# Loading a 4 KB input through the ACT queue, so that the SP queue begins with the first weights

## The chip, the cores and the metric

One core of one Trainium2 chip. The metric is the device time of one execution in microseconds (us). In the profile, PE multiplies matrices, VectorE (DVE), ACT and POOL compute, and SP and ACT issue transfers (loads), each into a queue of its own, called its ring below. Sixteen DMA engines carry them out in packets; here a packet is one row of a load, or the small mark that says it is complete. A semaphore is a counter on which an engine waits until a load or another engine has raised it. The kernel before takes 1297.78 us (median of 6 runs beside the changed kernel, 1297.59 to 1297.96).

## The reference

A decode step with one new token for each of four sequences: layernorm of x (4 x 512), an attention block over a cache, and a SwiGLU feed-forward block, all summed.

```python
xn = _layernorm(x, axis=-1)
q = (xn @ wq).reshape(B, Sq, H, Dh).transpose(0, 2, 1, 3)        # B 4, Sq 1, H 32, Dh 128
p = softmax(einsum("bhqd,bhkd->bhqk", q, k_cache) * Dh ** -0.5)   # 8192 keys for each head
a = einsum("bhqk,bhkd->bhqd", p, v_cache)...reshape(B, Sq, H * Dh) @ wo
return x + a + (silu(xn @ w_gate) * (xn @ w_up)) @ w_down
```

The caches are 2 x 4 x 32 x 8192 x 128 in bf16, some 537 MB. Each is read once, so the work is a long read from memory.

## The kernel before

The parts that matter, with cuts marked by `# ...`. `load_k` and `load_v` take 2 MB each, into one of nine buffers of a ring.

```python
x_sb = persist.tile([B, D], dt.bfloat16, name="x_sb")
nc.sync.dma_start(out=x_sb[:], in_=x_flat[:, :])
wq_v = A_wq.rearrange("(p c) n -> p c n", c=EC)
wq_t = []
for c2 in range(0, EC, 2):                       # two loads of 2 MB
    t_ = slot()
    nc.sync.dma_start(out=t_[:].rearrange("p (c n) -> p c n", c=2), in_=wq_v[:, c2:c2 + 2, :])
    wq_t.append(t_)
# ...
load_k(0)
load_k(1)
# ... ident, ident_f
for z_ in zq:
    nc.gpsimd.memset(z_[:], 0.0)                 # two long fills on POOL
# ...
nc.vector.tensor_copy(out=xf[:], in_=x_sb[:])    # the first use of x
# ... layernorm on VectorE, with one square root on ACT
nc.scalar.activation(out=std[:], in_=vsum[:], func=ACT.Sqrt, bias=epst[:, 0:1], scale=1.0 / D)
# ... transpose of xn; q = xn @ wq, first with wq_t[0], then with wq_t[1]
for i in range(M + LP + 1):                      # M = 128 pairs of head and sequence
    if i + 2 < M:
        load_k(i + 2)
    if 0 <= i + 2 - LP < M:
        load_v(i + 2 - LP, parts=4 if i + 2 - LP == M - 1 else 1)
    # ... scores of k tile i, softmax once a head, p @ v of tile i - 4
# ...
nc.sync.dma_start(out=out_flat[:, :], in_=res[:])
```

## Time and profile before

| | before |
|---|---|
| time, median | 1297.78 us |
| span of the profiled run | 1295.9 us |
| bytes read by DMA | 550.8 MB |
| DMA rate in the middle slices | some 430 GB/s |
| busy: PE, VectorE, ACT | 85%, 54%, 4% |
| first issue of wq on SP | 1.16 us |
| first wq data | 2.14 us |
| output issued by SP | 1293.59 us |

The first wq data are read from the DMA rate in slices of 0.02 us: a slice counts the packets that start in it, and the first that shows 16 KB packets starts at 2.14:

```profile
2.12:2.14 0.02, 0.00 (x0) 0.00 (x0) 0.02 (x1) 0.00 (x0) 0.02 (x1) 1.00 0.00 0
2.14:2.16 0.02, 0.00 (x0) 0.00 (x0) 0.02 (x1) 0.00 (x0) 0.02 (x1) 1.00 14.57 3277
```

### The profile page before, as it was taken

The page shows a single profiled execution, that of the slowest core. Times are in us where ns is not written, and L with a number is a line of the kernel's source. Part 1 is how long each engine was busy: PE and PEld are TensorE (multiplying, and loading weights), DVE is VectorE, ACT ScalarE, POOL GpSimd, SP SyncE. Part 2 cuts the span into 40 slices and gives each one's busy share as a digit, 9 for nine tenths or more (in the row PEclk, how much of TensorE's full clock was granted, in tenths as well). Part 3 has the DMA queues.
Part 4 walks back from the last instruction along what each step waited for, and adds up shares of the span by engine and source line. Part 5 has one row for each costly group of instructions (what it writes and reads, how often), then busy time and mean ns, then how long its engine had stood idle before and what let it go on. Part 6 is the DMA issues. An engine that isn't in the chain of part 4 may idle for free.

```text
span 1295.9 us, 11245 instructions
## 1 busy us (share of the span) xinstructions
PE 1095.1 (85%) x4676; PEld 423.2 (33%) x4676; DVE 693.3 (54%) x887; ACT 48.5 (4%) x102; POOL 5.6 (0%) x11
## 2 busy tenths in 40 slices
PE   5889888888888888888888888888888888886987
PEld 2343333333333333333333333333333333332333
DVE  7635554554554565555565455555555555544542
ACT  1000000000000000000000000000000000000000
POOL 1000000000000000000000000000000000000000
PEclk8989999999999999999999999999989989998999
DMA  9999999999999999999999999999999999999997
GB/s 396 429 430 432 431 429 431 431 431 430 430 432 430 430 430 431 431 429 432 432 428 429 434 430 429 431 431 431 431 431 431 430 430 431 430 403 419 432 429 305
DMA packets 42210, 551.49 MB, mean 426 GB/s; under 512 B 4264, under 2 KB 8368, under 8 KB 8880
## 3 DMA queue, kind: packets, MB, share of 16 engines
q1 hardware_dynamic: 42160, 550.79, 99.6%
q8 instruction: 36, 0.59, 0.2%
q14 instruction: 14, 0.11, 0.0%
HBM read 550.77 MB, written 0.00 MB: 425 GB/s over the span
## 4 chain that ended last, share of the span: by engine, by line
DMA 91%; PE 5%; DVE 3%; issue 0%; SPq 0%; ACT 0%; DVEq 0%; ACTq 0%
DMA slot<-in_A_k_cache_dram 86%; DMA slot<-in_B_w_up_dram 3%; DVE kt L256 3%; DMA slot<-in_A_v_cache_dram 3%; PE oacc L74 2%; PE sps L74 2%; PE mps L74 1%; PE xps L74 0%; SPq L97 0%; PE mps L278 0%; SPq L89 0%; DVE mx L272 0%; DVE res L388 0%; DVE yfx L227 0%; ACT o_sb L313 0%
## 5 line engine op out<-in xcount | busy, mean ns | idle before, releaser
L256 DVE STREAM_TRANSPOSE kt<-slot 128x1024 uint32<-128x1024 uint32 x512 | 593.5, 1212 | 284.8 <-DMA slot<-in_A_k_cache_dram 284.8
L74 PE MATMUL sps<-kt,zq 128*128 128x512 bf16 x2048 | 572.1, 416 | 179.0 <-DVE kt L256 165.6
L74 PEld LDWEIGHTS <-zq 128*128 128x128 bf16 x2048 | 208.8, 103 | 532.0 <-issue 361.4
L302 DVE RECIPROCAL rcp<-mps 128x4 f32<-128x4 f32 x32 | 5.8, 183 | 160.9 <-PE mps L74 160.9
L272 DVE TENSOR_REDUCE mx<-sps 128x1 f32<-128x512 f32 x32 | 22.1, 692 | 45.1 <-PE sps L74 45.1
L281 DVE TENSOR_REDUCE nm<-mps 128x4 f32<-128x64 f32 x32 | 7.2, 225 | 50.0 <-PE mps L278 50.0
L74 PE MATMUL xps<-ident_f,o_sb 128*128 128x4 f32 x256 | 33.1, 253 | 0.7 <-ACT o_sb L313 0.7
L74 PEld LDWEIGHTS xps<-ident_f,o_sb 128*128 128x128 f32 x256 | 31.1, 192 | 1.2 <-ACT o_sb L313 1.2
L247 DVE COPY zq<-qt 32x16 bf16<-32x16 bf16 x128 | 23.5, 183 | 1.3
L322 DVE TENSOR_TENSOR otn<-xps,rcp 128x4 bf16<-128x4 f32 x32 | 5.2, 162 | 34.1 <-PE xps L74 34.1
L313 ACT COPY o_sb<-oacc 128x512 f32<-128x512 f32 x32 | 18.7, 585 | 20.6 <-PE oacc L74 20.5
L74 PE MATMUL oacc<-slot,pt__1952 128*4 128x512 bf16 x64 | 14.6, 379 | 0.0
L74 PE MATMUL oacc<-slot,pt__3394 128*4 128x512 bf16 x64 | 14.6, 379 | 0.0
L74 PE MATMUL oacc<-slot,pt__6498 128*4 128x512 bf16 x64 | 14.6, 379 | 0.0
L74 PE MATMUL oacc<-slot,pt__922 128*4 128x512 bf16 x64 | 14.6, 379 | 0.0
L74 PE MATMUL oacc<-slot,pt__2158 128*4 128x512 bf16 x64 | 14.6, 379 | 0.0
L74 PE MATMUL oacc<-slot,pt__3188 128*4 128x512 bf16 x64 | 14.6, 379 | 0.0
L74 PE MATMUL oacc<-slot,pt__4424 128*4 128x512 bf16 x64 | 14.6, 379 | 0.0
L74 PE MATMUL oacc<-slot,pt__5248 128*4 128x512 bf16 x64 | 14.6, 379 | 0.0
L74 PE MATMUL oacc<-slot,pt__6282 128*4 128x512 bf16 x64 | 14.6, 379 | 0.0
L74 PE MATMUL oacc<-slot,pt__371 128*4 128x512 bf16 x64 | 14.6, 379 | 0.0
L74 PE MATMUL oacc<-slot,pt__1128 128*4 128x512 bf16 x64 | 14.6, 379 | 0.0
(204 smaller groups left out, 636.8 us busy)
## 6 DMA issues: line engine op xcount, KB each, us to landing
slot<-in_A_k_cache_dram SPq DMA_DIRECT2D x128, 2048.0 KB, 38.4
slot<-in_A_v_cache_dram SPq DMA_DIRECT2D x127, 2048.0 KB, 38.8
slot<-in_A_wq_dram SPq DMA_DIRECT2D x2, 2048.0 KB, 9.4
slot<-in_A_wo_dram SPq DMA_DIRECT2D x2, 2048.0 KB, 28.8
slot<-in_A_v_cache_dram SPq DMA_DIRECT2D x4, 512.0 KB, 28.0
slot<-in_B_w_gate_dram SPq DMA_DIRECT2D x1, 1792.0 KB, 38.2
slot<-in_B_w_up_dram SPq DMA_DIRECT2D x1, 1792.0 KB
slot<-in_B_w_down_dram SPq DMA_DIRECT2D x1, 1792.0 KB, 34.0
```

The source lines that it names most:

```text
L74: nc.tensor.matmul(out_ap, lhsT=lhsT, rhs=rhs, start=start, stop=True, skip_group_check=True, **kw)
L247: nc.vector.tensor_copy(out=zq[h % 2][a * QB:(a + 1) * QB, :, :, XO + a * QB].rearrange("p b (j r) -> p r j b", r=2), in_=qt[a * QB:(a + 1 ...
L256: nc.vector.transpose(out=kt[:].bitcast(dt.uint32).rearrange("p (j t r) -> p t j r", j=2, r=QB), in_=src.rearrange("p (t j r) -> p t j r", ...
L272: nc.vector.reduce_max(out=mx[:], in_=s_ps[h][:], axis=AX.X)
L281: nc.vector.tensor_reduce(out=nm[:], in_=mps[:, 0:P].rearrange("p (a x g r) -> p x a g r", a=NQ, x=B, r=2)[:, :, :, :, 0], axis=AX.XY, op= ...
L302: nc.vector.reciprocal(out=r_[:], in_=mps[:, P:P + B])
L313: nc.scalar.copy(out=o_sb[:], in_=o_acc[h % 2][:])
L322: nc.vector.tensor_tensor(out=otn[:, h, :], in0=xps[:], in1=rcp.pop(h)[:], op=ALU.mult)
```

## The change

The intent: SP issues its loads one after the other, and x is the first of them. The ACT queue issues nothing, and ACT isn't needed before the square root. If ACT issues x, SP can begin at once with wq, and the long stream starts sooner.

```diff
     x_sb = persist.tile([B, D], dt.bfloat16, name="x_sb")
-    nc.sync.dma_start(out=x_sb[:], in_=x_flat[:, :])
+    nc.scalar.dma_start(out=x_sb[:], in_=x_flat[:, :])
     wq_v = A_wq.rearrange("(p c) n -> p c n", c=EC)
```

## The prediction

> **What bounds the kernel now.** I began with the page's busy rows and its rows of 40 slices. The columns of the first line are engine, busy us, share of the span, instructions.
>
> ```profile
> PE 1095.1 (85%) x4676; PEld 423.2 (33%) x4676; DVE 693.3 (54%) x887; ACT 48.5 (4%) x102; POOL 5.6 (0%) x11
> ...
> DMA  9999999999999999999999999999999999999997
> GB/s 396 429 430 432 431 429 431 431 431 430 430 432 430 430 430 431 431 429 432 432 428 429 434 430 429 431 431 431 431 431 431 430 430 431 430 403 419 432 429 305
> ```
>
> No compute engine is full in every slice, but the DMA row is, at some 430 GB/s throughout. Only the first slice (396), two near the end (403, 419) and the last (305) fall short. Next the queues and the chain that ended last:
>
> ```profile
> q1 hardware_dynamic: 42160, 550.79, 99.6%
> ...
> DMA 91%; PE 5%; DVE 3%; issue 0%; SPq 0%; ACT 0%; DVEq 0%; ACTq 0%
> ```
>
> One queue carries 550.79 MB, which at 430 GB/s is 1281 us of the 1295.9 us span. The chain agrees: 91% of it is transfers. So the end is: the moment at which the data begin to flow, plus about 1281 us of stream with its few dips, plus a tail of compute. Is the stream always fed? A 2048 KB load takes a median 38.4 us from issue to landing; eight such loads at 431 GB/s need 8 x 2.097 MB / 431 GB/s = 38.9 us. So about eight loads are always outstanding, and a late issue must be later than the whole backlog before it costs anything. The list of each engine's instructions shows the same: SP's loads go round eight completion semaphores, and each waits for the one eight before it.
>
> Last, the first microseconds of the queue that the change touches (start, length, engine, line, operation):
>
> ```profile
> 0.74 0.36 SPq L84 DMA_DIRECT2D x_sb<-in_A_x_dram  x1
> 1.16 0.83 SPq L89 DMA_DIRECT2D slot<-in_A_wq_dram  x2
> 2.03 2.48 SPq L97 DMA_DIRECT2D slot<-in_A_k_cache_dram  x5
> 4.55 0.48 SPq L106 DMA_DIRECT2D slot<-in_A_v_cache_dram  x1
> 12.98 0.33 SPq L97 DMA_DIRECT2D slot<-in_A_k_cache_dram  x1
> ```
>
> and what the DMA engines moved then (the last two columns are DMA share and GB/s):
>
> ```profile
> 1.60:1.70 0.10, 0.00 (x0) 0.00 (x0) 0.10 (x1) 0.10 (x1) 0.10 (x1) 1.00 0.03 10
> 1.70:1.80 0.10, 0.00 (x0) 0.00 (x0) 0.10 (x1) 0.10 (x1) 0.10 (x2) 1.00 0.10 31
> ...
> 2.00:2.10 0.10, 0.00 (x0) 0.00 (x0) 0.07 (x1) 0.01 (x1) 0.10 (x1) 1.00 0.00 0
> 2.10:2.20 0.10, 0.00 (x0) 0.00 (x0) 0.09 (x2) 0.00 (x0) 0.10 (x1) 1.00 3.77 819
> ```
>
> The 4 KB of x pass between 1.6 and 1.8 us: 10 and 31 GB/s over 0.1 us each are 1 + 3.1 KB. The first wq data come in the slice that starts at 2.10 us, 0.94 us after that load's issue began at 1.16. Before 2.1 us the sixteen DMA engines do nothing but x. The only thing between the start and the stream that this kernel could shorten is SP's first issue.
>
> **What the Trainium skill says.** "DMA: Bandwidth & Descriptors", section "Issuing engines are not separate DMA queues", says that starting transfers from several engines only saves the sequencer's issue time, "which is usually small relative to the DMA itself". The trace gives that time: wq's issue starts 0.42 us after x's (1.16 - 0.74). That is all that this page promises here.
>
> The same page, section "Queues, rings and completion order", says that SP and ACT each have a ring on each of the same sixteen engines, and that an engine takes turns between rings packet by packet. Before, all data are on one ring, so this trace can't show it; it matters for when x lands once wq is on the other ring.
>
> "SBUF — State Buffer", section "SBUF: two separate sides", says that VectorE and GpSimd share a port pair which one instruction locks for its whole length. The trace agrees:
>
> ```profile
> 1.75 4.34 POOL L121 MEMSET zq<- 128x2528 bf16 x2
> ...
> 2.11 4.15 DVE L134 TENSOR_SCALAR rowb_q<-rowb 128x4 f32<-128x4 f32 x1
> 2.19 4.33 DVE L138 CAST xf<-x_sb 4x512 f32<-4x512 bf16 x1
> 6.55 0.67 DVE L140 TENSOR_REDUCE xsum<-xf 4x1 f32<-4x512 f32 x1
> ```
>
> An operation on 128x4 elements takes 4.15 us, and it ends just after POOL's two fills do (1.75 + 4.34 = 6.09). The cast that reads x stands behind it until 6.5.
>
> "ScalarE: Activation LUTs", section "What ACT_TABLE_LOAD costs", gives about 1283 ns for a table load; ACT's first instruction here is one of 1.28 us at 0.73.
>
> **The change part by part.** The compiled orders of the two kernels differ in one instruction: x's load leaves the head of SP's list and enters at the head of ACT's. PE, VectorE and POOL have the same lists, and the semaphores are numbered as before.
>
> *Removed from SP:* one issue, 0.36 us plus a gap of 0.06 us. wq's first load starts at 0.74 instead of 1.16, and if the same 0.94 us to the first data hold, the stream starts at about 1.68 instead of 2.10 us. The seven loads behind it move by the same 0.42 us: -0.42 us on the path.
>
> *Added to ACT:* one issue at 0.73, some 0.4 us by SP's figure. The table load moves from 0.73 to about 1.15 and ends at about 2.4 us. ACT's next work is the square root, which starts at 9.37 after 7.36 us of waiting for VectorE. So 0.0 us on the path.
>
> *x beside wq:* four rows of 1 KB no longer have the engines to themselves. An engine that has a 16 KB packet of wq ahead of x keeps it waiting for that packet. As an estimate from the rate, 16 KB at 431/16 = 27 GB/s is 0.6 us; twice, for the data and the completion mark, 1.2 us. So x lands between about 1.9 and 3.1 us. The cast can't begin before the port is free at 6.1, so the layernorm doesn't move at all. x's own bytes delay the stream by 4 KB of 550 MB.
>
> *The projection q:* its first half waits for layernorm (11.04 us), its second for the second wq load (13.24 us, a wait of 0.30 us). With wq 0.42 earlier, that wait goes and PE is 0.30 us earlier at most. The buffers of wq are then free up to 0.3 us sooner. At 12.98, when the first of them is refilled, about 16.8 MB have been issued and 4.5 MB moved ((12.98 - 2.5) us x 430 GB/s), so 28 us of backlog lie ahead. This gain doesn't reach the end.
>
> *Cross-queue wait:* the first v load (at 4.55) waits for the semaphore of x, eight loads back, before and after alike. It would be issued at 4.13, after x has landed by the estimate above. Even if it waited some us, seven loads (14.7 MB, 34 us) are queued by then.
>
> Sum: -0.42 us on a stream whose later course is a function of its start. 1297.76 - 0.42 = 1297.34 us, or -0.03%.
>
> **The tail** moves with the stream:
>
> ```profile
> 1251.39 32.78 DMA slot<-in_A_v_cache_dram
> 1284.17 0.04 issue
> 1284.21 6.23 PE oacc L74 x32
> ```
>
> PE waits for the last but one v and then works without a pause to the end at 1295.9. Nothing in it depends on the first microseconds but through the landing.
>
> **The rivals.**
> 1. *The stream does not start earlier.* The two issuers could go through one descriptor generator one after the other, so that wq's data still come some 0.4 us after x's. The traces so far have one issuer and can't exclude it. For it: both issues would begin within 0.01 us of each other. Against it: nothing in the profile. Then 1297.7 us.
> 2. *x lands late and layernorm becomes the path.* If x waited for several packets on its ring, say until 9 us, the cast would start 3 us later and q with it. The profile speaks against a cost even then: x is first used at 6.1, and a q that is 3 us later would delay refills that have about 28 us of backlog in hand. VectorE and PE work off the queued k tiles between 19.5 and 33 us and then wait for data again (0.31 us at 34.17); 3 us more would be made up a few tiles later, as VectorE is only 54% busy. Then still 1297.3 to 1297.8 us.
> 3. *The stream shifts against the clock's throttling or the two wo loads.* SP is held for 29.5 us in one issue near 1131 us, and the rate falls there (403 and 419 GB/s). If the earlier start moves what collides there, the time moves by a part of a us or one us either way. Against: the three runs before lie within 0.21 us, so this dip is reproduced. 1296.5 to 1298.5 us.
>
> **Range and chances.** I give the first rival one chance in four: 0.75 x (-0.42) + 0.25 x 0 = -0.3, so 1297.4 us. The three runs spread by 0.2 us; I allow about 1 us either way for the third rival and for another execution: 1296.5 to 1298.3. Two per cent are 26 us, sixty times the issue that is moved. Nothing in the profile is near that, so within 2% has 0.98.
>
> **What would show it right or wrong.** In the profile after: the first wq issue at about 0.74 and its first data at about 1.7 us (at 2.0 or later, rival one); the issue of x on ACT near 0.73, and the table load ending near 2.4; the cast still ending near 6.5 and the square root near 9.4 (if later, rival two); the same eight loads in flight with 38.4 us to landing; the wait of PE for the last but one v ending near 1283.8 instead of 1284.2, and a span of about 1295.5. Wrong would be a rate outside 429 to 432 GB/s in the middle slices, or a time that differs from 1297.8 by more than 1 us: either would mean that a second ring in use costs or gives something over the whole stream, which no line above shows.

## The result, and the profile after

The changed kernel takes 1297.30 us (median of 6 runs, 1297.22 to 1297.43), 0.48 us under the kernel before. The ratio is 0.9996 (95% interval 0.9984 to 1.0009). A ratio here is the mean time of one kernel's runs over that of the other's of the same rounds, so not quite the ratio of the medians. The interval is wider than the effect, but the runs themselves do not overlap: the slowest of the changed kernel (1297.43) is under the fastest of the kernel before (1297.59).

The page of the changed kernel, rates in 40 slices and queues:

```profile
GB/s 399 431 429 431 430 429 430 433 430 430 431 430 430 429 432 430 429 432 430 430 430 431 431 429 431 430 430 432 430 430 431 431 430 429 432 402 421 429 430 306
...
q1 hardware_dynamic: 42152, 550.79, 99.7%
...
q10 hardware_dynamic: 8, 0.00, 0.0%
```

The stream is the same, with 399 for 396 in the first slice and the same two dips near the end (402 and 421). The second ring, q10, carries eight packets: the four rows of x and their four completion marks.

The timeline of the changed kernel in its first microseconds (start, length, engine, line, operation):

```profile
0.73 0.56 ACTq L84 DMA_DIRECT2D x_sb<-in_A_x_dram  x1
...
0.74 0.88 SPq L89 DMA_DIRECT2D slot<-in_A_wq_dram  x2
...
1.33 1.28 ACT L150 ACT_TABLE_LOAD   x1 [1.33 <-PEq L404]
...
2.19 4.34 DVE L138 CAST xf<-x_sb 4x512 f32<-4x512 bf16 x1
...
9.38 0.29 ACT L150 ACTIVATE std<-vsum,epst 4x1 f32<-4x1 f32 x1 [6.76 <-DVE vsum L148]
...
11.04 3.90 PE L74 MATMUL sps<-slot,xnt_w 128*32 128x512 bf16 x32 [0.33 <-DVE xnt_w L160]
```

wq's issue starts at 0.74 instead of 1.16. The cast of x still ends at 6.53, behind POOL's fills, and the square root still starts at 9.4. The 32 matmuls of q now run without the break before the second half of wq.

The DMA rate in two slices of 0.02 us of the changed kernel (the last number is GB/s):

```profile
1.74:1.76 0.02, 0.00 (x0) 0.00 (x0) 0.02 (x1) 0.02 (x1) 0.02 (x2) 1.00 0.17 51
1.76:1.78 0.02, 0.00 (x0) 0.00 (x0) 0.02 (x1) 0.02 (x1) 0.02 (x2) 1.00 3.35 819
```

In such slices, the rows of x (51 GB/s) pass at 1.66 to 1.76, as before, and the first wq packet comes at 1.76 instead of 2.14: 0.38 us sooner. The chain of waits at the end of the changed kernel (start, length, what):

```profile
1251.04 32.78 DMA slot<-in_A_v_cache_dram
1283.82 0.04 issue
1283.87 6.23 PE oacc L74 x32
```

The last but one v is issued at 1251.04 instead of 1251.39 and takes the same 32.78 us; PE starts its last work at 1283.87 instead of 1284.21. So 0.38 us at the start of the stream are still 0.35 us after 1250 us.

### The profile page after: what moved, and what is told of

Same layout as the page of the kernel before. It is cut to its first block, busy times and chain, and to the rows that moved or that the text cites. A ratio compares the mean times of both kernels' runs of the same rounds, so it can differ in the third digit from the quotient of the medians.

```text
span 1295.6 us, 11245 instructions
## 1 busy us (share of the span) xinstructions
PE 1096.1 (85%) x4676; PEld 423.6 (33%) x4676; DVE 693.1 (54%) x887; ACT 48.7 (4%) x102; POOL 5.6 (0%) x11
## 4 chain that ended last, share of the span: by engine, by line
DMA 89%; PE 7%; DVE 3%; issue 0%; SPq 0%; ACT 0%; DVEq 0%; ACTq 0%
DMA slot<-in_A_k_cache_dram 84%; PE oacc L74 3%; DVE kt L256 3%; DMA slot<-in_B_w_up_dram 3%; PE sps L74 3%; DMA slot<-in_A_v_cache_dram 3%; PE mps L74 1%; PE xps L74 0%; SPq L97 0%; PE mps L278 0%; SPq L89 0%; DVE mx L272 0%; DVE res L388 0%; DVE yfx L227 0%; DVE otn L322 0%
## 6 DMA issues: line engine op xcount, KB each, us to landing
slot<-in_A_wo_dram SPq DMA_DIRECT2D x2, 2048.0 KB, 29.4
```

## The experiments

Nine kernels, 5 rounds each. The kernel before ran beside each call, with medians of 1297.78, 1297.78 and 1297.70 us over 9 runs each. All results were correct. The theory: **the time is the start of the wq stream plus a constant, as long as loads are always outstanding.**

### The changed kernel again

No edit.

> The changed kernel once more, as the yardstick of this chip. Theory (the time is the start of the wq stream plus a constant): 0.4 to 0.5 us under the kernel before. Rival (the difference of 0.48 us on record is spread between executions): anywhere within 0.2 us of the kernel before.

Measured 1297.39 us (1297.30 to 1297.45), 0.39 us under the kernel before, ratio 0.9997. It is the yardstick for the rest. Its gain lies nearer to the 0.38 us of the trace than the 0.48 us of the first comparison, so the 0.1 us between them is spread.

### x on SP, but behind wq

```diff
-    nc.sync.dma_start(out=x_sb[:], in_=x_flat[:, :])
     # ... after the loop that loads wq
+    nc.sync.dma_start(out=x_sb[:], in_=x_flat[:, :])
```

> x stays on the SP queue but is issued behind both wq loads, so it lands behind 4.2 MB, at some 11 to 12 us, and layernorm and q come about 5 us later than in the changed kernel. Theory: the stream starts at 1.7 us as in the changed kernel and the late q is hidden by the backlog; time within 0.15 us of the changed kernel (0.3 to 0.5 us under the kernel before; x's issue now lies in the shadow of data). Rival A (the second ring itself gives the gain): no gain, equal to the kernel before. Rival B (layernorm and q are on the path): 4 to 5 us slower than the changed kernel.

Measured 1297.44 us (1297.24 to 1297.59): the gain is there without ACT's queue, so it comes from the order and not from a second ring. In the timeline of this run, VectorE waits for x and begins its cast at 12.94 us:

```profile
12.94 0.42 DVE L138 CAST xf<-x_sb 4x512 f32<-4x512 bf16 x1 [6.67 <-DMA x_sb<-in_A_x_dram]
```

Rival B falls: the cast ends 6.8 us later (13.36 instead of 6.53) and q's last cast starts 6.5 us later (24.36 instead of 17.82), and it costs nothing that can be told from the spread.

### Three more loads in front, on SP and on ACT

```diff
+    for i in range(3):
+        x_d = persist.tile([B, D], dt.bfloat16, name=f"x_d{i}")
+        nc.sync.dma_start(out=x_d[:], in_=x_flat[:, :])      # the other kernel: nc.scalar, for these and x
     nc.sync.dma_start(out=x_sb[:], in_=x_flat[:, :])
```

> Three more loads of x, into tiles that nobody reads, stand on the SP queue ahead of x and wq. Theory: wq's first issue moves from 1.16 to about 2.4 us (three times 0.42), the stream starts at about 3.4, and the time is 1.25 us over the kernel before. Rival (the start of the stream is hidden further on, or only the generator's latency counts): under 0.4 us over the kernel before.

> The same three extra loads, but on the ACT queue with x. Theory: wq's first issue stays at 0.74 us and its data at 1.7; ACT's table load ends some 2 us later, long before 9.4; time within 0.15 us of the changed kernel. Rival (both issuers share one descriptor generator, so issues of one delay the other): wq's data or the later loads come later and the time rises by up to 1.25 us over the changed kernel.

On SP: 1298.55 us (1298.45 to 1298.82), 0.77 us over the kernel before. On ACT: 1297.20 us (1297.15 to 1297.36), 0.19 us under the changed kernel. The timeline of the run on SP:

```profile
0.74 1.01 SPq L86 DMA_DIRECT2D x_d<-in_A_x_dram  x3
1.79 0.29 SPq L87 DMA_DIRECT2D x_sb<-in_A_x_dram  x1
2.13 0.83 SPq L92 DMA_DIRECT2D slot<-in_A_wq_dram  x2
```

Four issues of the same load take 1.39 us (2.13 - 0.74), 0.35 each and not 0.42, and the first wq packet comes at 3.12, 0.98 later than before. The dose has the right sign and nearly the right size, but 0.77 is not 0.98, and on ACT the time fell where it should have stayed. In both, some 0.2 us is missing. The traces show where, in the table below: up to the issue of the output all follow the start of the stream.

| kernel | first wq packet | output issued by SP | from the one to the other | from output issue to the last record |
|---|---|---|---|---|
| before | 2.14 | 1293.59 | 1291.45 | 2.28 |
| changed | 1.76 | 1293.24 | 1291.48 | 2.30 |
| changed, again | 1.76 | 1293.24 | 1291.48 | 2.30 |
| x behind wq | 1.74 | 1293.41 | 1291.67 | 2.29 |
| three more on SP | 3.12 | 1294.65 | 1291.53 | 2.10 |
| three more on ACT | 1.74 | 1293.26 | 1291.52 | 2.11 |

From the first wq packet to the output's issue it is 1291.45 to 1291.67 us, over starts that differ by 1.38 us. This is the theory, measured. The rest, some 0.2 us, lies after the output's issue. There the packed trace records five looks of SP at semaphores (instructions that go on when the semaphores have their values), some 0.063 us apart, one of which waits for the output to land. The last record is taken by its start. In the kernel before and the changed one it is the first of the five, so four follow the landing; with three more loads it is the fourth, and one follows. Three looks are 3 x 0.063 = 0.19 us.

The run on ACT shows another thing, in VectorE's timeline:

```profile
8.81 0.42 DVE L141 CAST xf<-x_sb 4x512 f32<-4x512 bf16 x1 [2.54 <-DMA x_sb<-in_A_x_dram]
```

x was issued at 1.95 us, as the fourth on its ring, when wq's packets were already flowing. VectorE could begin at 8.8: some 6.9 us for 4 KB. The packets of each ring (count, MB, share; `prof four_on_act --dma --window`), first from 2.45 to 5.50 us and then from 5.50 to 8.30:

```profile
q1 hardware_dynamic: 64, 1.05, 80.9%
...
q1 hardware_dynamic: 93, 1.26, 105.6%
q10 hardware_dynamic: 24, 0.01, 1.5%
```

In the first stretch only SP's ring (q1) moved; why ACT's ring (q10) stood is not shown. In the second, all 24 packets of three loads on ACT's ring passed, x as the last of them. In the changed kernel x goes ahead of wq's first packet. In this run SP's k issues also ended 5 us late (9.15 instead of 4.19), at no cost: the first packet counts, and not these issues.

### How late x may be

```diff
     load_k(0)
     load_k(1)
+    nc.sync.dma_start(out=x_sb[:], in_=x_flat[:, :])   # the other kernel: behind load_k(0) to load_k(4)
```

In the other kernel load_k(2) to load_k(4) are moved up from the main loop. The order of SP's loads, but for x, stays the same.

> x on the SP queue behind both wq loads and two k loads, so it lands near 22.6 us (12.9 us behind two loads, plus two more at 4.85) and q is ready near 34 us instead of 18. Theory (only the start of the stream counts while the backlog lasts): k5 is then issued near 29.5 us, when some 12 us of loads are still outstanding, so the time stays within 0.2 us of the changed kernel (about 1297.4). Rival (the margin is smaller than the backlog says, because buffers come free too slowly while VectorE catches up): 1 to 8 us slower.

> x behind all five k loads as well, so it lands near 37 us and k5 is issued near 44 us, 3 to 4 us after the eight loads before it have run out near 41 us. Theory: a gap of about 4 us in the DMA traffic near 41 us, and the time about 4 us over the changed kernel, 1300.5 to 1302.5 us. Rival (even this is absorbed): 1297.4 us. Rival (the pipeline never regains its depth): more than 5 us slower.

Behind two k loads: 1297.34 us (1297.33 to 1297.40). x lands at 22.6 us, q is late by 16 us (its last cast starts at 33.90), and nothing is lost. Behind five: 1304.46 us (1304.25 to 1305.45), ratio 1.0053, 7.1 us over the changed kernel where 3 to 5 were expected. The rates in stretches of this run:

```profile
30.00:40.00 10.00, 0.00 (x0) 0.00 (x0) 2.66 (x6) 0.00 (x0) 0.00 (x0) 1.00 1.01 433
41.00:45.00 4.00, 3.19 (x32) 1.32 (x36) 0.59 (x2) 0.00 (x0) 0.00 (x0) 1.00 0.03 12
45.00:60.00 15.00, 9.97 (x70) 4.34 (x64) 13.80 (x16) 3.21 (x3) 0.00 (x0) 0.77 1.02 407
60.00:80.00 20.00, 15.89 (x53) 5.54 (x53) 15.30 (x21) 0.78 (x2) 0.00 (x0) 0.83 1.01 429
80.00:100.00 20.00, 18.34 (x80) 6.96 (x79) 14.48 (x17) 0.00 (x0) 0.00 (x0) 1.00 0.94 359
100.00:130.00 30.00, 26.55 (x185) 13.48 (x187) 8.16 (x14) 1.58 (x4) 0.00 (x0) 0.89 1.01 432
```

The gap near 41 us is there as foreseen: four us at 12 GB/s, and 15 us at 407. Against 430 GB/s that is 3.9 + 0.8 = 4.7 us. The second loss was not foreseen: 20 us at 359 GB/s, another 3.3 us. The sum, 8.0 us, is nearly the 8.1 us by which the profiled run (1305.45, the slowest of the five) lies over the changed kernel's (1297.36). What SP waited for between 45 and 110 us in this run:

```profile
SPq L105 <- PE oacc L74: 17.4, 3, 6.7
SPq L105 <- DVE kt L256: 9.9, 2, 5.8
SPq L96 <- DVE kt L256: 8.7, 2, 4.6
SPq L200 <- DVE kt L256: 7.6, 1, 7.6
SPq L201 <- PE mps L74: 6.1, 1, 6.1
SPq L199 <- DVE kt L256: 4.9, 1, 4.9
```

and the same stretch of the changed kernel:

```profile
SPq L97 <- DMA slot<-in_A_k_cache_dram: 8.0, 3, 4.6
SPq L97 <- DMA slot<-in_A_v_cache_dram: 5.7, 3, 3.6
```

In the slow kernel every wait, 58 us in all, is ended by a compute engine. In the changed kernel the longest, and some 37 of 61 us, are for the landing of an earlier load; the rest are for compute there too. After about 100 us the rate is back. So once the backlog is gone, the loss is more than the gap itself. That buffers come free late until about 100 us is read from these waits; no run tests it alone.

### The looks at the end

```diff
     nc.scalar.dma_start(out=x_sb[:], in_=x_flat[:, :])
+    for i in range(4):                                        # the other kernel: 5
+        x_d = persist.tile([B, D], dt.bfloat16, name=f"x_d{i}")
+        nc.scalar.dma_start(out=x_d[:], in_=x_flat[:, :])
```

> The changed kernel with four more loads of x on the ACT queue, behind the real one. The extra loads move the output's load number round the eight completion semaphores from the fourth to the eighth. Theory (at the end SP looks through the eight semaphores in order, 0.063 us each, and those behind the output's come after its landing): four fewer to go, 0.25 us under the changed kernel, about 1297.15. x goes first on its queue and its cast still ends near 6.5 us. Rival (the 0.2 us between the runs with extra loads and the changed kernel was chance, or comes with any extra load): equal to the changed kernel, or the same as with three extra loads (1297.2).

> As before with five extra loads: the output's semaphore is then the first of the eight. Theory: seven to go after its landing instead of four, 0.19 us over the changed kernel, about 1297.6, although it has one load more than the run beside it that should be the fastest. Rival (any extra load shortens the end, or chance): 1297.2, no more than the run with four extra.

With four: 1297.22 us (1297.17 to 1297.31), 0.17 under the yardstick (of another call, with the same median of the kernel before) instead of 0.25. With five: 1297.38 us (1297.17 to 1297.46), like the changed kernel and not 0.19 over it. The second expectation failed. Two things can be read from the traces, in the same way as above:

| kernel | looks that follow the one for the output | from output issue to the last record | first wq packet to output issue |
|---|---|---|---|
| changed | 4 | 2.30 | 1291.48 |
| three more on ACT | 1 | 2.11 | 1291.52 |
| four more on ACT | 0 | 2.05 | 1291.55 |
| five more on ACT | 2 | 2.15 | 1291.72 |

Fewer looks after the landing, a shorter end: three, four and two fewer give 0.19, 0.25 and 0.15 us, where 0.063 each would give 0.19, 0.25 and 0.13. But with the output on the first of the eight semaphores two looks follow, not seven: there are five looks in all and not eight, each at two semaphores, and the output's is in the third. With five more loads, the first k load on SP has to wait for x's semaphore (a wait of 0.6 us; the issue starts at 2.22 instead of 1.65), and the stretch up to the output is 0.24 us longer than in the changed kernel; whether the one comes from the other is not shown. The run with four more beats the changed kernel by 0.17 us with loads that nobody reads. It is a measurement and no improvement to keep.

### The other small packets: wo on ACT

```diff
-        nc.sync.dma_start(out=t_[:].rearrange("p (h e) -> p h e", h=n),
+        nc.scalar.dma_start(out=t_[:].rearrange("p (h e) -> p h e", h=n),    # wo, 2 x 2 MB in rows of 1 KB
```

on top of the changed kernel, because SP is held behind these two loads and the rate is low there. SP's timeline in the changed kernel:

```profile
1127.32 0.39 SPq L236 DMA_DIRECT2D slot<-in_A_wo_dram  x1
1131.18 29.71 SPq L97 DMA_DIRECT2D slot<-in_A_k_cache_dram  x1
...
1161.46 0.39 SPq L236 DMA_DIRECT2D slot<-in_A_wo_dram  x1
1161.93 14.25 SPq L97 DMA_DIRECT2D slot<-in_A_k_cache_dram  x1
```

An issue normally takes 0.33 us; the k load behind each wo load takes 29.71 and 14.25.

> The changed kernel with the two wo loads on the ACT queue as well. On SP a k load behind each of them is held for 29.7 and 14.25 us in its issue, and the DMA rate falls to 339 to 393 GB/s in parts of 1155 to 1180 us. Theory (SP's hold is hidden by the loads in flight; what is lost there comes from the 4096 packets of 1 KB, 46 ns each, 11.8 us for what 431 GB/s would do in 9.7, some 2 us): the loss stays, 1296.6 to 1297.4 us. Rival (the hold itself costs: a second queue that takes it off SP gains it): 2 to 3 us faster, near 1294.5 us. Second rival: ACT is held instead, its exponentials come late and the refills with them: 1 to 10 us slower.

Measured 1301.12 us (1301.06 to 1301.73), ratio 1.0028, 3.7 us over the yardstick. The loss came, but neither of the expected mechanisms is it. The issues of wo in the page of the changed kernel:

```profile
slot<-in_A_wo_dram SPq DMA_DIRECT2D x2, 2048.0 KB, 29.4
```

and in that of this run (last column: median us to landing):

```profile
slot<-in_A_wo_dram ACTq DMA_DIRECT2D x2, 2048.0 KB, 68.4
```

with what PE, and then SP, waited for around it:

```profile
PE yo_ps L74 <- DMA slot<-in_A_wo_dram: 18.0, 1, 18.0
...
SPq L97 <- DMA slot<-in_A_wo_dram: 32.1, 1, 32.1
```

On its own ring, wo takes 68 us instead of 29 to land. The packets of each ring (count, MB, share) in this run between 1135 and 1180 us (`prof wo_on_act --dma --window 1135:1180`):

```profile
q1 hardware_dynamic: 1232, 17.99, 93.4%
q10 hardware_dynamic: 1232, 1.26, 7.9%
```

The counts are equal, as when the rings take turns packet by packet, so 1.26 MB of wo in rows of 1 KB pass beside 17.99 MB of k and v in rows of 16 KB. PE then stands 18 us before wo. SP waits 32.1 us for the first wo load, since each load waits for the one eight before it, and later 18.7 us for the second. The rate falls to 337 to 400 GB/s between 1185 and 1200 us, when rows of 1 KB are most of the packets, and to 249 and 217 between 1210 and 1220, around the end of SP's second wait. As an estimate against 430 GB/s, the last gap loses 4.6 us; the stretch of small rows loses 2.5 us, where the changed kernel loses 2.9 (25 us at 380). That makes 4.2 us, against 3.7 measured.

The hold of the issuer moved with wo: SP's issues beside it took 0.33 us each, and ACT's second issue took

```profile
1147.18 19.39 ACTq L236 DMA_DIRECT2D slot<-in_A_wo_dram  x1
```

So the second rival was right that ACT is held and that the time grows, but not about the way: ACT's exponential at 1146.13 starts 0.1 us after its place in the changed kernel (1146.02), and the next one, at 1205.67, is late because it waits for VectorE's result, after PE's wait.

## Why the prediction was right

The time was foreseen as 1297.4 and measured as 1297.30 and 1297.39. The 1297.4 is a mean that gives rival one a quarter; the sum itself said 0.42 us less, and 0.48 and 0.39 were measured. That the mean lies nearer to the second measurement is chance. By the prediction's own steps:

1. **What bounds the kernel**: right. The stretch from the first wq packet to the output is 1291.45 to 1291.53 us in the kernel before, the changed one and both kernels with three more loads, while the start moves over 1.38 us.
2. **Removed from SP, -0.42 us**: right in kind; the first packet moved by 0.38. From the start of wq's issue to its first packet it is 0.98 us before (2.14 - 1.16) and 1.02 after (1.76 - 0.74); the prediction took 0.94 for both, from slices of 0.1 us.
3. **Added to ACT, 0.0 us on the path**: right. The issue took 0.56 us, not 0.4, and the table load ends at 2.61 instead of 2.4; the square root didn't move. Why the issue took longer beside SP's than the 0.36 us before is not tested.
4. **x beside wq, landing by 3.1 us**: the time was not affected, but the estimate of 1.2 us of delay was wrong where x really meets wq. In the changed kernel x is ahead and meets nothing; with three more loads on ACT it took 6.9 us. The sizing failed on "twice, for the data and the completion mark": it has neither the 3.1 us in which only SP's ring moved nor the turns of the loads ahead on x's own ring.
5. **q 0.30 us earlier at most, and not at the end**: right; 0.15 us (q's last cast starts at 17.82 instead of 17.97).
6. **Backlog of 28 us**: borne out. x landing at 22.6 us makes q 16 us late and costs nothing; landing at 37 it makes q 31 us late (its last cast starts at 48.45) and costs 7.1.
7. **Rival one**, at one in four, fell: wq's data come 0.38 us sooner. **Rival two**'s statement that a late q is made up is true up to 22.6 us. **Rival three** was not seen: the two dips are 402 and 421 GB/s after, 403 and 419 before.
8. **Readings that were off**, without effect on the sum: the sign "outside 429 to 432 GB/s" was drawn too tight, as the kernel before itself shows 428 and 434 in single middle slices (and the changed one 433). "Numbered as before" is not quite so: in the packed traces semaphores 100 and 101 have changed places.

What the prediction did not hold is the end of the program. It plays no part in this comparison, as in both kernels four looks follow the output's. That it differs by 0.2 us between kernels that differ in the number of loads would have been read as an effect of the start, had the traces not been compared piece by piece.

## What to carry to other kernels

When one stream of transfers fills the whole span, an issue ahead of it costs its own length once, and nothing else of the start matters as long as loads are outstanding: put the small first load behind the big ones or on another queue, and expect tenths of a microsecond. Before moving a small transfer to a second queue, ask what flows on the first one at that moment: it was free for 4 KB that went first, cost 6.9 us of latency for 4 KB that came just behind, and 3.7 us of the kernel's time for 4 MB in rows of 1 KB. For effects of 0.03%, compare pieces between fixed events of the traces, since ends of programs differ by as much.

## What the Trainium skill lacked or had wrong

- "DMA: Bandwidth & Descriptors", section "Queues, rings and completion order", says that an engine switches rings per packet, "≈9-17 descriptors typical". Beside a ring of 16 KB rows, the rings changed after each packet that the profile lists, one row or completion mark (1232 of each ring in 45 us). The page doesn't say what this does to a ring of small rows: landing in 68.4 us instead of 29.4 for 2 MB, and 6.9 us for 4 KB.
- The same page, section "Issuing engines are not separate DMA queues", says that issuing from several engines only saves the sequencer's time. For x that is so (0.38 us). For wo it was not only that: the same bytes from ACT cost 3.7 us.
- The same page, section "Latency and other measured facts", gives about 600 ns to the first byte for this kind of queue, without saying from when. From the start of the issue it was 0.98 to 1.02 us for wq here and 0.92 for x in the kernel before (1.66 - 0.74); from the end of x's issue (1.10) it was 0.56, near the page's figure.
- No page says for how long an issue can be held behind a load of many rows (it would belong to "Perfetto Trace Analysis", section "DMA Instruction — HWDGE (DVE, Sync)"): SP was held 29.7 and 14.25 us behind the two wo loads of 2048 rows each, and ACT 19.39 us when they were on its queue.
- No page that was read tells of the looks at semaphores after the output's landing at the end of the program: 0.063 us each, none to four of them in these kernels.
